# A fused attention and expert kernel: GpSimd's transfers stand behind a small copy of each unit's first quarter of h, and half of the last expert's second weights are reloaded

## The chip, the cores and the metric

The kernel runs on one core of a Trainium2 chip. The metric is the device time of one execution in microseconds (us); a lower one is better. The engines are named as in the profile: PE (TensorE, matmuls), PEld (TensorE's weight loads), DVE (VectorE), ACT (ScalarE), POOL (GpSimd) and SP (SyncE, which here only issues DMAs).

## What is computed

The reference is attention followed by a mixture of experts over the same 4608 tokens (8 sequences of 576, 8 heads of 64, so 512 features a token). Attention looks back over a window of 128 with a linear bias by distance. Then, with x the attention's output:

```python
P = np.exp(x @ w_gate - max)
for _ in range(8):                     # Sinkhorn balance
    P /= P.sum(1, keepdims=True) + 1e-09
    P /= P.sum(0, keepdims=True) + 1e-09
    P *= N / E
for e in range(8):
    h = np.maximum(x @ w1[e], 0.0)     # 512 -> 1024
    out += P[:, e:e + 1] * (h @ w2[e]) # 1024 -> 512
```

Every expert works on every token; P only weights.

## The kernel before

**First stage** (to about 320 us). Attention runs, and in its gaps PE computes experts 0 and 1 for all tokens. Their results y go to DRAM (`ysp`, 36 blocks of 128 tokens for each of the two experts), and so does x (`xd`).

**Second stage** (about 320 us to the end). Experts 2 to 7 run over 18 groups of two token blocks each (256 tokens). One group and one expert make a unit: 108 units, `N`, in the order of `units` (line 905), six (`NE`) to a group. The order of groups is 0 to 7, then 16 and 17 (the tails of the sequences, 64 tokens of each), then 8 to 15.

A unit's first layer (L983, `part`) uses seven block products in place of eight (Strassen): parts a11, s1, s2, a12, s3, s4, a22 accumulate in the PSUM banks A, B and C, and ACT and DVE carry sums between the banks. The result h, [256 tokens x 1024], comes out in four quarters. Quarter 0 is ready after a12 (ACT's relu, L1021, from bank A), quarter 3 after "p+" and quarter 1 after "c+" (DVE's add L1035, then ACT's relu), quarter 2 after a22. Quarters 0 and 3 lie side by side in one of three rotating buffers `hr`, and 1 and 2 in another. One DMA transpose of each pair, `turn_h` (L1027), brings h into `hs` with features on the partitions; SP issues it after p+ and after a22. The buffers called s5y in the profile include the third of the rotation.

The second layer is also a seven-product scheme. DVE adds quarters of the transposed h (L1051, tokens t5 t6 t1 t4 t7), and PE runs the products (L1079, token X) for the unit before, into the banks `psM` (L1079, M in the text). After a group's last unit the products are added to `acc` by DVE (L1123, tokens g1 to g7), in the first units of the next group.

**The written-out order.** All engines work in program order. `plans` (L1250) gives one line of tokens for each of a group's six units; `first` (L1258) replaces the line for some units at the start and for the last unit, N-1. `step` (L1207) reads the tokens. Those that matter here:

- XL0, XL1 (L1236): GpSimd loads the next group's x of block 0 or 1 from `xd` into `xst`. Both blocks share one buffer, which the profile calls consts.
- XT0, XT1 (L919): SP transposes that x into the next group's `xset`.
- Y00, Y01, Y10, Y11 (L1092): GpSimd loads y of expert 0 or 1 (first digit) and block 0 or 1 (second) from `ysp`.
- B00 to B11 (L1097 for expert 0, L1101 for expert 1), "begin": DVE starts acc of a block with P times y, or adds the second y.
- FIN (L1131, L1135): GpSimd stores both blocks of acc of the group before: two stores of 256 KB, or four of 128 KB for a tail group.
- SX (L934 to L936): DVE forms the sums of the next group's x.
- W, F: left-over sums of weights and products of the first stage.

So y loads have one buffer `y[0]`, except y of expert 1 and block 1, which goes to `xst` (`y_at`, L1088). A y load therefore waits for the begin that read the buffer, and XL waits for the XT that read `xst`.

Expert 7's second weights `W2L[7]["all"]` lie in one tile [128, 8 rows of f, 512]. The seven-product scheme overwrites two of their four quarters by sums: q12 (first four f rows, right half) becomes f6, and q21 (last four, left half) f7. The last unit N-1 has no product stream behind it; it ends with ordinary products (`plain`, L1137), which need the original weights. So after expert 7's last Strassen unit the whole tile is loaded again, a f row at a time (`load_w2`, L618), three after each of the units 103 and 104 and two after 105 (L1279).

Of the kernel before, what the change touches and what calls it, by code (L numbers as in the profile page):

```python
# [9 lines left out]
FP16 = mybir.dt.float16  # L10
# [4 lines left out]
def kernel(  # L15
# [10 lines left out]
    nc = tc.nc  # L26
# [17 lines left out]
    SM = RI * P  # L44
    TL = S - SM
# [19 lines left out]
    per = ctx.enter_context(tc.tile_pool(name="per", bufs=1))  # L65
# [186 lines left out]
    if True:  # L252
# [343 lines left out]
        HB = HD // 2  # L596
        NF2 = NFT // 2
# [18 lines left out]
        def load_w2(e, n=0, of=1):  # L616
            k = NFT // of
            nc.gpsimd.dma_start(  # L618
                out=W2L[e]["all"][:, n * k : n * k + k, :],
                in_=moe_w2[e].rearrange("(ft p) d -> p ft d", p=P)[:, n * k : n * k + k, :],  # L620
            )
# [49 lines left out]
        def some(n):  # L671
            for _ in range(min(n, len(todo))):
                todo.pop(0)()
# [44 lines left out]
        for n, (b, kb, u) in enumerate(steps):  # L718
# [111 lines left out]
            if 10 * b + at >= 66:  # L830
                i = 10 * b + at - 66
# [72 lines left out]
        groups = [*range(8), 16, 17, *range(8, 16)]  # L904
        units = [(g, e) for g in groups for e in range(2, E)]
        N = len(units)
        NE = E - 2
# [4 lines left out]
        acc = per.tile([P, 2, HD], FP32, name="acc", tag="xT", bufs=4)  # L912
        xst = [acc.rearrange("p m d -> p (m d)").bitcast(FP16)[:, HD * i : HD * i + HD] for i in range(2)]
# [16 lines left out]
        B11, B21, B12, B22, T1, T3, T2, T4 = range(8)  # L930
# [79 lines left out]
        def rows(n, i):  # L1010

            return hr[(2 * n + i) % 3]

        def quarter(n, slot):
            return rows(n, AT[slot] // 2)[:, AT[slot] % 2]
# [17 lines left out]
        def add_h(n, slot, name):  # L1033
            to = quarter(n, slot)
            nc.vector.tensor_tensor(out=to, in0=psum(name), in1=s5, op=ALU.add)  # L1035
            relu(n, slot, to)
            if slot == 3:
                turn_h(n, 0)

        def sum_h(n, to):  # L1040
            if n < 0:
                return
            t = hs[n % 2]
            x, y, op = {
                5: (1, 3, ALU.add),
                6: (1, 0, ALU.subtract),
                1: (0, 3, ALU.add),
                4: (0, 2, ALU.add),
                7: (3, 2, ALU.subtract),
            }[to]  # L1050
            nc.vector.tensor_tensor(out=t[:, AT.get(to, to)], in0=t[:, AT[x]], in1=t[:, AT[y]], op=op)  # L1051
# [3 lines left out]
        RIGHT = {1: "f1", 2: "q11", 3: "f3", 4: "f4", 5: "q22", 6: "f6", 7: "f7"}  # L1055
        BANK = {3: (0, 0), 4: (0, 1), 2: (1, 0), 6: (1, 1), 5: (2, 0), 7: (2, 1), 1: (3, 0)}
        Ms: dict = {}

        def sum_of(g, m):
            bk = (4 * groups.index(g) + BANK[m][0]) % 5  # L1060
            if bk not in Ms:
                if bk < 4:
                    Ms[bk] = mps.tile([P, 2, 2 * P], FP32, name=f"psM_{bk}")
                else:
                    Ms[bk] = psum("M").rearrange("p (h n) -> p h n", h=2)
            return Ms[bk][:, BANK[m][1], :]
# [6 lines left out]
        def product():  # L1073
            n, m = stream.pop(0)
            g, e = units[n]
            half = BANK[m][1]
            ps = sum_of(g, m)
            for f in range(NF2):
                nc.tensor.matmul(  # L1079
                    out=ps,  # L1080
                    lhsT=hs[n % 2][:, LEFT[m], f, :],
                    rhs=W2L[e][RIGHT[m]][:, f, :],
                    start=(e == 2 and f == 0 and half == 0),
                    stop=(ends(n) and f == NF2 - 1 and (half == 1 or m == 1)),
                    skip_group_check=True,
                )

        def y_at(e, m):  # L1088
            return xst[0] if e == m == 1 else y[0]

        def load_y(g, e, m):
            nc.gpsimd.dma_start(out=y_at(e, m), in_=ysp[e, 2 * g + m])  # L1092
# [29 lines left out]
                    a, p2 = q4[:, lo, :], ps  # L1122
                nc.vector.tensor_tensor(out=a, in0=a, in1=p2, op=op)  # L1123

        def finish(g):
            for m in range(2):
                blk = 2 * g + m
                a = acc[:, m, :]
                if blk < 4 * B:
                    t0 = S * (blk // 4) + P * (blk % 4)  # L1130
                    nc.gpsimd.dma_start(out=out[t0 : t0 + P, :], in_=a)  # L1131
                else:
                    for half in range(2):
                        t0 = S * (2 * (blk - 4 * B) + half) + SM
                        nc.gpsimd.dma_start(out=out[t0 : t0 + TL, :], in_=a[TL * half : TL * half + TL])  # L1135

        def plain(m, name, fh, lo, hi):  # L1137

# [68 lines left out]
        def step(n, plan):  # L1207
            gi = n // NE
            for tok in plan.split():
                if tok == "X":  # L1210
                    product()
                elif tok == "W":
                    some(1)
                elif tok == "F":
                    filler.take()
                elif tok == "p+":
                    add_h(n, 3, "B")
                elif tok == "c+":
                    add_h(n, 1, "C")
                elif tok[0] == "t":  # L1220
                    sum_h(n - 1, int(tok[1]))
                elif tok[0] == "g":
                    last = gi if n == N - 1 else gi - 1
                    if last >= 0:
                        gather(groups[last], int(tok[1]))
                elif tok[0] == "B":
                    begin(groups[gi], int(tok[1]), int(tok[2]))
                elif tok == "FIN":
                    if gi > 0:
                        finish(groups[gi - 1])  # L1230
                elif tok in ("XT0", "XT1"):
                    if gi + 1 < len(groups):
                        turn_x2(gi + 1, int(tok[2]))
                elif tok in ("XL0", "XL1"):
                    if gi + 1 < len(groups):
                        nc.gpsimd.dma_start(out=xst[int(tok[2])], in_=xd[2 * groups[gi + 1] + int(tok[2])])  # L1236
                elif tok == "SX":
                    if gi + 1 < len(groups):
                        sums_x(gi + 1)
                elif tok[0] == "Y":  # L1240
                    load_y(groups[gi], int(tok[1]), int(tok[2]))
                elif tok[0] == "L":
                    slot = int(tok[1])
                    plain_l1(n, slot, {0: "A", 3: "B", 1: "C", 2: "B"}[slot])
                    if slot > 1:
                        turn_h(n, 3 - slot)
                else:
                    part_of(n, tok)

        plans = (  # L1250
# [6 lines left out]
        )  # L1257
        first = {  # L1258
# [4 lines left out]
            N - 1: "a11 X s1 s2 a12 B11 X s3 s4 p+ c+ X X a22 X t5 X X t6 t1 t4 g3 X t7 X g4 X g2 X g6 X g1 g5 g7",  # L1263
        }
        sums_at = {1: 3, 2: 3, 3: 3, 4: 4, 5: 4, 6: 3, 9: 4, 10: 3}
        for n in range(N):
            plan = first.get(n, plans[n % NE])
            one, rest = plan.split(" ", 1)
            step(n, one + " W" * sums_at.get(n, 0) + " " + rest)
            if n == 1:  # L1270
                store()
                aux = per.tile([P, 4, NF2, HB], FP16, name="aux", tag="w2t", bufs=2)
                w2f = per.tile([P, 4, NF2, HB], FP16, name="w2f", tag="w1t", bufs=2)
                todo += sums_of(6, F1_6, w2f[:, 2], w2f[:, 3])
                todo += sums_of(7, aux[:, 0], w2f[:, 0], w2f[:, 1]) + quads_w1(6) + quads_w1(7)
                y.append(per.tile([P, HD], FP16, name="y_e", tag="yo", bufs=YO))
                xst[:] = [consts.rearrange("p a n -> p (a n)").bitcast(FP16)] * 2
                step(n, "Y00 XL0")
            if N - NE + 1 <= n < N - 2:  # L1279
                for i in range(3 * (n - N + NE - 1), min(8, 3 * (n - N + NE))):  # L1280
                    load_w2(E - 1, i, 8)
        plain(1, "A", 1, 0, HD)
        plain(0, "C", 0, 0, HB)
        plain(0, "B", 0, HB, HD)
# [33 lines left out]
```

## Time and profile before

| | us |
|---|---|
| median of 3 timed runs | 1002.11 |
| lowest and highest | 1001.25, 1004.09 |
| the profiled execution | 998.06 |
| its span, first to last instruction | 996.3 |
| PE busy | 979.4 |
| DVE busy | 687.3 |
| ACT busy | 625.5 |
| POOL busy | 192.6 |

The profile shows one execution. A line of a timeline has the start, the time from start to the end of the group of like instructions, the engine, the line of the kernel, what it writes and reads, how many, and in square brackets how long the engine was idle before it and what ended that. A stretch's line has its length, each engine's busy time with the number of its instructions, the granted TensorE clock, the busy share of the 16 DMA engines and the GB/s. In the chain that ended last each piece is named by the engine or DMA that it was spent on. Issue to landing is the time from a DMA's issue to its completion.

In all, 216 transposes of h (SP; `hs<-hr` 144 with a median of 3.3 us to landing, `hs<-s5y` 72 with 3.2), 34 of x from xst (2.6), 72 loads of y (54 with 3.0 and 18 with 2.5), 34 loads of x (2.5), 38 stores (30 of 256 KB with 2.9, 8 of 128 KB with 3.2) and 8 reloads of w2 (128 KB as written, 5.2) are in the second stage.

### The profile page before, as it was taken

The numbers are of one execution on the slowest core, as the hardware profiler recorded it, in microseconds if no ns is written. First come the engines' busy times: TensorE is split into PE (matmuls) and PEld (weight loads), VectorE is DVE, ScalarE is ACT, GpSimd is POOL, SyncE is SP. The second block draws the span as 40 slices with busy tenths as digits, with TensorE's granted clock in tenths as the row PEclk, the third lists the DMA queues.
The fourth block names the chain that finished last, engine by engine and source line by source line (L and its number), as shares of the span: only waits on it lengthen the run. The fifth ranks groups of instructions, "written<-read, shape, count | busy, mean of one in ns | idle before, by whom it ended". The sixth has DMA issues, their size and how long they took to land.

```text
span 996.3 us, 19438 instructions
## 1 busy us (share of the span) xinstructions
PE 979.4 (98%) x7247; PEld 626.0 (63%) x7247; DVE 687.3 (69%) x1546; ACT 625.5 (63%) x1000; POOL 192.6 (19%) x353
## 2 busy tenths in 40 slices
PE   7999999999999999999999999999999999999997
PEld 5645665566544566666666666666666666666665
DVE  5736677675688797676676676676676676776766
ACT  7654555554434656676677677676677676767663
POOL 3315444354010001001111101111101101101120
PEclk9999999999999999999999999999999999999999
DMA  9998999989997667666656656666667656655675
GB/s 244 217 276 208 192 239 224 224 186 185 225 196 159 117 112 145 121 117 148 132 113 138 136 126 131 136 116 128 124 127 133 138 126 129 138 123 122 143 130 119
DMA packets 383454, 155.55 MB, mean 156 GB/s; under 512 B 335296, under 2 KB 372928, under 8 KB 383360
## 3 DMA queue, kind: packets, MB, share of 16 engines
q1 hardware_dynamic: 359680, 110.87, 55.0%
q0 software_dynamic: 23248, 43.27, 20.2%
q8 instruction: 57, 0.93, 0.4%
q14 instruction: 37, 0.30, 0.1%
q10 hardware_dynamic: 432, 0.16, 0.1%
HBM read 78.30 MB, written 23.59 MB: 102 GB/s over the span
## 4 chain that ended last, share of the span: by engine, by line
PE 88%; DMA 6%; DVE 3%; ACT 1%; issue 1%; SPq 1%; POOL 0%; DVEq 0%; POOLq 0%; ACTq 0%
PE psM L1079 30%; PE psB L983 13%; PE psy L159 12%; PE psh L137 9%; PE psA L983 8%; PE psC L983 8%; PE psh L118 3%; DMA hs<-s5y 2%; PE psN L491 1%; PE psS L457 1%; DMA xset<-consts 1%; DMA v<-in_v_dram 1%; DMA consts<-ysp 1%; DVE pt L468 1%; ACT psB L1196 0%
## 5 line engine op out<-in xcount | busy, mean ns | idle before, releaser
L1079 PEld LDWEIGHTS <-hs 128*128 128x128 f16 x2996 | 292.4, 98 | 127.6 <-DVE hs L1051 2.6
L983 PEld LDWEIGHTS <-xset 128*128 128x128 f16 x1484 | 144.8, 98 | 94.0 <-issue 3.8
L1051 DVE TENSOR_TENSOR hs<-hs 128x512 f16<-128x512 f16 x535 | 194.3, 418 | 8.9 <-DMA hs<-hr 4.7
L1079 PE MATMUL psM<-w2l,hs 128*128 128x256 f16 x1440 | 195.6, 273 | 1.2 <-DVE hs L1051 1.2
L159 PE MATMUL psy<-w2t,hT 128*128 128x512 f16 x576 | 135.7, 379 | 0.0
L1021 ACT ACTIVATE hr<-hr,L_sb 128x512 f16<-128x512 f16 x142 | 98.4, 716 | 59.1 <-DVE hr L1035 57.8
L1079 PE MATMUL psM<-more,hs 128*128 128x256 f16 x864 | 121.0, 273 | 1.8 <-DMA hs<-hr 1.8
L1035 DVE TENSOR_TENSOR hr<-psB,s5y 128x512 f16<-128x512 f32 x71 | 49.0, 691 | 94.0 <-PE psB L983 93.2
L983 PE MATMUL psB<-s,xset 128*128 128x512 f16 x356 | 105.7, 378 | 0.8 <-ACT psB L1196 0.4
L983 PE MATMUL psA<-w1l,xset 128*128 128x512 f16 x356 | 105.9, 379 | 0.0
L149 ACT ACTIVATE hT<-psh 128x512 f16<-128x512 f32 (+1 forms) x104 | 60.4, 581 | 70.0 <-PE psh L137 69.9
L137 PE MATMUL psh<-xT,w1t 128*128 128x512 f16 (+1 forms) x448 | 99.0, 364 | 0.0
L463 ACT ACTIVATE pt<-psS 128x1024 f16<-128x1024 f32 x64 | 64.6, 1022 | 49.9 <-PE psS L457 49.3
L159 PEld LDWEIGHTS <-hT 128*128 128x128 f16 x576 | 54.1, 98 | 58.9 <-issue 1.4
L1200 ACT COPY psC<-psB 128x512 f32<-128x512 f32 x106 | 60.4, 570 | 48.8 <-PE psB L983 48.2
L582 DVE CAST yo<-psy 128x512 f16<-128x512 f32 x65 | 44.5, 689 | 50.9 <-PE psy L159 50.3
L1123 DVE TENSOR_TENSOR acc<-acc,psM 128x256 f32<-128x256 f32 (+1 forms) x162 | 77.1, 503 | 2.9 <-PE psM L1079 0.2
L1196 ACT COPY psB<-psA 128x512 f32<-128x512 f32 x106 | 60.4, 570 | 25.9 <-PE psA L983 24.4
L468 DVE TENSOR_TENSOR pt<-pt,mask 128x1024 f16<-128x1024 f16 x64 | 52.1, 814 | 30.4 <-ACT pt L463 30.4
L1198 ACT COPY s5y<-psC 128x512 f32<-128x512 f32 x106 | 62.7, 591 | 6.5 <-PE psC L983 6.5
L137 PEld LDWEIGHTS <-w1t 128*128 128x128 f16 x448 | 41.3, 98 | 37.5 <-issue 0.6
L1131 POOL DMA_DIRECT2D out_dram<-acc x30 | 16.3, 548 | 247.0 <-DVE acc L1123 247.0
(141 smaller groups left out, 1324.0 us busy)
## 6 DMA issues: line engine op xcount, KB each, us to landing
ysp<-yo SPq DMA_DIRECT2D x65, 128.0 KB, 4.2
v<-in_v_dram SPq DMA_DIRECT2D x32, 256.0 KB, 5.0
out_dram<-acc POOLq DMA_DIRECT2D x30, 256.0 KB, 2.9
y_e<-ysp POOLq DMA_DIRECT2D x54, 128.0 KB, 3.0
q<-in_q_dram SPq DMA_DIRECT2D x5, 1024.0 KB, 7.9
k<-in_k_dram SPq DMA_DIRECT2D x5, 1024.0 KB, 9.9
consts<-xd POOLq DMA_DIRECT2D x34, 128.0 KB, 2.5
w1t<-in_moe_w_dram POOLq DMA_DIRECT2D x3, 1024.0 KB, 11.0
```

What stands on the lines that cost most here:

```text
L137: nc.tensor.matmul(out=ps[:, 0:nt], lhsT=w1ts[e][:, dt, P * ft : P * ft + P], rhs=xT[:, at : at + nb, dt, :], start=(dt == 0), stop=(dt == ...
L149: nc.scalar.activation(out=st["hT"][:, ft, 0:nt], in_=ps[:, 0:nt], func=AF.Relu)
L159: nc.tensor.matmul(out=ps, lhsT=st["hT"][:, ft, P * ms : P * ms + P], rhs=w2ts[e][:, ft, :], start=(ft == 0), stop=(ft == NFT - 1),)
L463: nc.scalar.activation(out=pt, in_=ps.rearrange("p a y n -> p (a y) n"), func=AF.Exp, scale=scale)
L468: nc.vector.tensor_tensor(out=pt, in0=pt, in1=mask_of[kb][:, 4 * u : 4 * u + 4, :], op=ALU.mult)
L983: nc.tensor.matmul(out=psum(name), lhsT=xset[n // NE % 2][:, x, P * k : P * k + P], rhs=q[k], start=(start and k == 0), stop=(k == 1), ski ...
L1021: nc.scalar.activation(out=quarter(n, slot), in_=src, func=AF.Relu, scale=P_sb[:, blk, e : e + 1])
L1051: nc.vector.tensor_tensor(out=t[:, AT.get(to, to)], in0=t[:, AT[x]], in1=t[:, AT[y]], op=op)
L1079: nc.tensor.matmul(out=ps, lhsT=hs[n % 2][:, LEFT[m], f, :], rhs=W2L[e][RIGHT[m]][:, f, :], start=(e == 2 and f == 0 and half == 0), stop= ...
L1123: nc.vector.tensor_tensor(out=a, in0=a, in1=p2, op=op)
L1196: nc.scalar.copy(out=psum("B"), in_=psum("A"))
L1198: nc.scalar.copy(out=s5, in_=psum("C"))
```

## The change

A new token G stands in the plans right after a12 in units 0 to 4 of a group (and in the special lines of the first group and the last unit). It is a copy on GpSimd of two elements of each partition from quarter 0 of this unit's h into a new tile `held_at`, which nothing reads. All of GpSimd's transfers of the second stage come right behind a G. The order over the group becomes: unit 0 x of block 0 and Y00; unit 1 x of block 1; unit 2 the store of block 0 (FIN0) and Y01; unit 3 Y10 and the store of block 1 (FIN1); unit 4 Y11. XT0 and XT1 stand behind a22 in units 0 and 1 (units 2 and 3 before). The begins stand in units 3, 4, 5 and 5. y of block 1 now goes to `xst` for both experts, and y of block 0 to `y[0]`. The loads that stood by themselves behind unit 1 are gone.

A new token R, of the last group alone, reloads one half f row of expert 7's second weights: the right half for the first four rows, the left half for the last four, which are the overwritten quarters. Two R stand in unit 1, one in unit 2, one in unit 3, two in unit 4 and two in the last unit. The rest of the tile isn't loaded again.

```diff
+        held_at = per.tile([P, 2], FP16, name="held_at")
...
         def y_at(e, m):
-            return xst[0] if e == m == 1 else y[0]
+            return xst[0] if m else y[0]
...
-        def finish(g):
-            for m in range(2):
-                blk = 2 * g + m
...
+        def finish(g, m):
+            blk = 2 * g + m
...
+        def gate(n):
+
+            nc.gpsimd.tensor_copy(out=held_at, in_=quarter(n, 0)[:, 0:2])
+
+        again = list(range(NFT))
+
+        def load_again():
+
+            ft = again.pop(0)
+            lo = HB if ft < NF2 else 0
+            nc.gpsimd.dma_start(
+                out=W2L[E - 1]["all"][:, ft, lo : lo + HB],
+                in_=moe_w2[E - 1].rearrange("(ft p) d -> p ft d", p=P)[:, ft, lo : lo + HB],
+            )
...
-                elif tok == "FIN":
+                elif tok in ("FIN0", "FIN1"):
                     if gi > 0:
-                        finish(groups[gi - 1])
+                        finish(groups[gi - 1], int(tok[3]))
+                elif tok == "G":
+                    gate(n)
+                elif tok == "R":
+                    if gi == len(groups) - 1:
+                        load_again()
...
         plans = (
-            "a11 s1 X X s2 X a12 s3 s4 p+ X c+ t5 t6 X a22 X t1 t4 X t7",
-            "a11 s1 X g4 X s2 g3 X a12 g6 s3 X s4 p+ X X c+ a22 g5 X t5 t7 g7 t6 t1 t4 g2 Y00 XL0",
-            "a11 s1 X s2 g1 FIN X X a12 s3 p+ s4 X c+ t5 X a22 XT0 XL1 t6 t1 X X t7 t4",
-            "a11 s1 X X s2 B00 Y01 X a12 s3 s4 p+ c+ t5 X t6 X t4 a22 X t1 X XT1 t7 B01",
-            "a11 Y10 Y11 s1 X X s2 X X a12 s3 p+ s4 c+ X t5 t6 t7 X t4 X a22 t1 SX B10",
-            "a11 X X s1 s2 a12 X X s3 B11 s4 p+ c+ X X X t5 t6 t4 t7 a22 t1",
+            "a11 s1 X X s2 X a12 G XL0 Y00 s3 s4 p+ X c+ t5 t6 X a22 XT0 X t1 t4 X t7",
+            "a11 s1 X g4 X s2 g3 X a12 G XL1 R R g6 s3 X s4 p+ X X c+ a22 XT1 g5 X t5 t7 g7 t6 t1 t4 g2",
+            "a11 s1 X s2 g1 X X a12 G FIN0 Y01 R s3 p+ s4 X c+ t5 X a22 t6 t1 X X t7 t4",
+            "a11 s1 X X s2 B00 X a12 G Y10 FIN1 R s3 s4 p+ c+ t5 X t6 X t4 a22 X t1 X t7",
+            "a11 s1 X X s2 B01 X X a12 G Y11 R R s3 p+ s4 c+ X t5 t6 t7 X t4 X a22 t1 SX",
+            "a11 X X s1 s2 B10 a12 X X s3 B11 s4 p+ c+ X X X t5 t6 t4 t7 a22 t1",
         )
         first = {
...
-            4: "L0 Y10 Y11 X X L3 X X L1 X t5 X t6 t4 L2 t7 t1 X SX B10",
-            5: "L0 X X L3 B11 X X L1 X t5 X t6 t4 L2 t7 t1 X",
-            N - 1: "a11 X s1 s2 a12 B11 X s3 s4 p+ c+ X X a22 X t5 X X t6 t1 t4 g3 X t7 X g4 X g2 X g6 X g1 g5 g7",
+            2: "a11 s1 X s2 X X a12 G Y00 XL0 s3 p+ s4 X c+ t5 X a22 XT0 t6 t1 X X t7 t4",
+            3: "a11 s1 X X s2 B00 X a12 G XL1 Y10 s3 s4 p+ c+ t5 X t6 X t4 a22 XT1 X t1 X t7",
+            4: "L0 X X B10 L3 X X L1 G Y01 X t5 X t6 t4 L2 t7 t1 X SX",
+            5: "L0 X X B01 L3 X X L1 G Y11 X t5 X t6 t4 L2 t7 t1 X B11",
+            N - 1: "a11 X s1 s2 B10 a12 G R R B11 X s3 s4 p+ c+ X X a22 X t5 X X t6 t1 t4 g3 X t7 X g4 X g2 X g6 X g1 g5 g7",
         }
...
-                step(n, "Y00 XL0")
-            if N - NE + 1 <= n < N - 2:
-                for i in range(3 * (n - N + NE - 1), min(8, 3 * (n - N + NE))):
-                    load_w2(E - 1, i, 8)
```

More of the change, by code (lines that the diff above doesn't have):

```diff
@@ L1123, in gather @@
                 nc.vector.tensor_tensor(out=a, in0=a, in1=p2, op=op)
-        def finish(g):
-            for m in range(2):
-                blk = 2 * g + m
[L1128 to L1135, printed above, removed]
+        def finish(g, m):
+            blk = 2 * g + m
+            a = acc[:, m, :]
+            if blk < 4 * B:
+                t0 = S * (blk // 4) + P * (blk % 4)
+                nc.gpsimd.dma_start(out=out[t0 : t0 + P, :], in_=a)
+            else:
+                for half in range(2):
+                    t0 = S * (2 * (blk - 4 * B) + half) + SM
+                    nc.gpsimd.dma_start(out=out[t0 : t0 + TL, :], in_=a[TL * half : TL * half + TL])
+        def gate(n):
[8 more added lines that the diff above has]
+            )
         def plain(m, name, fh, lo, hi):
```

## The prediction

> **What bounds the kernel now.** I read the page's engine shares, the chain that ended last, and then the busy times by stretch, because a mean over 996 us says little about one stage.
>
> ```profile
> span 996.3 us, 19438 instructions
> PE 979.4 (98%) x7247; PEld 626.0 (63%) x7247; DVE 687.3 (69%) x1546; ACT 625.5 (63%) x1000; POOL 192.6 (19%) x353
> PE 88%; DMA 6%; DVE 3%; ACT 1%; issue 1%; SPq 1%; POOL 0%; DVEq 0%; POOLq 0%; ACTq 0%
> ```
>
> PE is the bound: 88% of the chain, busy for 98% of the span, at a granted clock of 1.00. Only what PE loses to waits can be won. Where it loses them stands in the stretches of the second stage, cut at about one group of six units each (columns: stretch, its length, busy us of PE, PEld, DVE, ACT, POOL, clock, DMA share, GB/s):
>
> ```profile
> 396.00:432.60 36.60, 35.86 (x249) 23.94 (x247) 25.35 (x59) 25.42 (x43) 4.32 (x8) 1.00 0.73 130
> ...
> 542.00:578.50 36.50, 36.50 (x254) 24.59 (x252) 25.36 (x59) 25.77 (x42) 4.32 (x8) 1.00 0.61 130
> ...
> 651.50:688.00 36.50, 35.45 (x246) 23.68 (x244) 23.32 (x56) 24.35 (x41) 4.84 (x9) 1.00 0.69 127
> 688.00:726.20 38.20, 36.80 (x250) 24.03 (x248) 25.86 (x60) 25.51 (x42) 5.82 (x11) 1.00 0.67 121
> ```
>
> An ordinary group (542 to 578) has PE busy all 36.50 us: 6.08 us a unit, with nothing to win. The losses sit in a few places: about 432, 688 and 720, and the last group. In the timeline of PE the last one reads:
>
> ```profile
> 969.76 0.59 PE L983 MATMUL psB<-w1l,xset 128*128 128x512 f16 x2
> 972.18 1.05 PE L1079 MATMUL psM<-more,hs 128*128 128x256 f16 x8 [1.83 <-DMA hs<-hr]
> 973.07 0.59 PE L983 MATMUL psA<-w1l,xset 128*128 128x512 f16 x2
> 973.50 0.59 PE L983 MATMUL psC<-aux,xset 128*128 128x512 f16 x2
> 975.26 0.94 PE L1079 MATMUL psM<-w2l,hs 128*128 128x256 f16 x7 [1.17 <-DVE hs L1051]
> ```
>
> Two 512-column matmuls take 0.43 us from start to start (973.07 to 973.50), so the start at 972.18 is 1.99 us late and that at 975.26 is 1.33 late: 3.32 us. The same subtraction elsewhere: 0.75 at 431.06; 2.07 at 687.75, 689.11 and 691.65 together; 1.42 from 713 to 723.5; 0.58 at 394 and 397. Sum **8.14 us**. Some 1.0 us more (331, 334, 381, 632, 982) has no transfer in it, and I leave it.
>
> What makes these late, in the chain in order of time:
>
> ```profile
> 425.10 5.92 DMA hs<-s5y
> ...
> 682.26 5.42 DMA consts<-ysp
> ...
> 965.52 9.23 DMA hs<-s5y
> ```
>
> A transpose of h alone lands in 3.2 us (median 3.2 and 3.3). At 425 and 965 one took 5.92 and 9.23, with GpSimd's transfers beside it: in the last group two stores, five w2 loads and a y load issued from 962.52 to 968.0. At 682 a load of y, itself beside two transposes, held a begin on VectorE, behind which the sums for the next h stood. Slower transposes alone do no harm: in ordinary groups the second one of a unit lands after 4.8 us (500.19) and PE doesn't stop. Harm begins between 4.8 and 5.4 us.
>
> **The change, part by part.**
>
> *The gate.* Where is the gap it aims at? Stretches of two ordinary units, same columns:
>
> ```profile
> 485.70:487.40 1.70, 1.70 (x15) 1.24 (x13) 1.67 (x5) 1.70 (x3) 0.04 (x1) 1.00 0.87 308
> 487.40:488.80 1.40, 1.40 (x12) 0.97 (x11) 0.86 (x3) 1.01 (x3) 0.00 (x0) 1.00 0.98 185
> 488.80:490.20 1.40, 1.40 (x11) 0.86 (x10) 0.00 (x0) 0.65 (x2) 0.00 (x0) 1.00 0.99 187
> 490.20:491.00 0.80, 0.80 (x5) 0.35 (x4) 0.14 (x1) 0.65 (x1) 0.00 (x0) 1.00 0.73 168
> 491.00:493.00 2.00, 2.00 (x18) 1.59 (x17) 2.00 (x5) 1.46 (x4) 1.06 (x2) 1.00 0.00 0
> ```
>
> Two stores (issued 484.65 and 485.19) fill the DMA engines from 485.7 to 487.4: 1.05 us from issue to traffic, 0.85 us a store. The transposes issued at 486.25, 487.62 and 488.96 follow until 491.0. Then the DMA engines stand empty for 2 us. ScalarE's relu of the first quarter ends at 491.04 (start 490.35, 0.69), just there; the next transpose is issued at 492.33 and moves from about 493.45 (1.15 later, as 486.25 to 487.4). A gated transfer: relu end 491.04, a copy of two elements, issue at 491.2, traffic from 492.25. The second is issued 0.54 later (POOL's row of one issue) and moves from 492.8. Loads of 128 KB (half a store, about 0.45) and one store fit before 493.45. A third starts at 493.35, beside the transpose, for about 0.5 us: a transpose of 3.2 becomes 3.7, below 4.8. Cost at PE: 0.
>
> The copy itself has no row. Bounds: a memset of 128x16 takes 0.134 us, a copy of 64x512 took 0.60; I take 0.13, the row nearest in size. 90 units hold a gate, on an engine busy for 4.3 of 36.5 us a group: 0. At 0.60 the second transfer would lie half beside a transpose, still under 4.8. Its wait: behind the gate stand only GpSimd's transfers, for which VectorE's begins and the x transposes wait, 4 to 12 us later in the plans, against landings of 2.3 to 3. The buffer of h that it reads is next written by the "c+" of the following unit, some 6.5 us later: no wait.
>
> The Trainium skill speaks against this: "DMA: Bandwidth & Descriptors", Rules for kernel authors, says to issue a DMA early, compute, and wait late, and a gate issues later. By that rule the begins would wait longer; by the rows VectorE's wait for y (41.2 us, 17 times) comes from one y buffer reloaded behind each begin, and the sum goes by the rows. "SBUF — State Buffer" of the Trainium skill, Who interferes with whom, says that GpSimd reading SBUF and a VectorE operation with two SBUF inputs exclude each other; at the gate VectorE runs the adds with one input in PSUM (L1035), and none of the h sums until 492.06. By the rule a gate would lose one sum, 0.42 us, at the worst. No trace here shows it.
>
> *Loads spread and re-paired.* Before, second-block and second-expert y each followed a begin. Now Y00 has a slot three units ahead of its begin, Y01, Y10 and Y11 at least one unit (6.08 us). VectorE's 41.2 + 7.6 us of waits go; VectorE is off the path in ordinary groups, so that is worth only the part inside the 2.07, 1.42, 0.75 and 0.58. The stores are split over two units: the second block's begin then waits for a store issued in the unit before; VectorE reaches it at 493.8 in the unit of the rows above, a store issued at 491.7 lands at 494.6 (2.9), so it waits 0.8 us and is done at 495.1 (0.49), before the next add at 497.37: 0. XT0 and XT1 come two units earlier, behind the second transpose of h as now; SP's queue gets no longer. XL1 and Y01 can't be issued before the x transpose has left xst: 488.96 to 491.94, 2.98 us, which is 0.4 us before the next transpose of h. They are single transfers there, and just fit.
>
> *Tail groups (656 to 726).* Four half stores and a load crowded one unit; now two half stores and a load in each of two: three transfers, 3.7 us a transpose. Gain 2.07 + 1.42.
>
> *Reload of w2.* 8 loads of 64 KB (counted as written) instead of 8 of 128, at most two in a unit. In units 2 to 4 of the last group they are the third transfer: 3.7 us instead of 8 to 9. Gain 3.32. In the very last unit two are issued about 1.4 us before the transpose and land some 3 us later, 1 us before the plain products at 988.99 want them; a miss costs its own length, and I put 0.3 there.
>
> Sum against the profiled execution: 998.06 - 8.14 + 0.3, and 0.2 for third transfers: 990.4. The timed runs' median is 4.05 us longer than that execution. Nothing shows why; that they had more such stalls is possible (these vary from group to group), that it is another thing too, so the gain there is between 7.6 and 11.7. I take the middle, 9.6: **992.5**.
>
> **Rivals.**
> - *The stalls thin out only by half.* XL1 and Y01 go by the landing of an x transpose and not by the gate, with 0.4 us to spare; where one lands 0.5 late, load and transposes of h lengthen each other as at 425, and the third transfers add. For: the cascade at 672 to 688 began so. Against: twelve ordinary groups live with 4.8 us. Half of 8.1: 998.0.
> - *The change moves traffic without parting it*, as where GpSimd comes to its gate already late (plain units of the first group have their first quarter early, so the gate holds nothing). As many bytes beside transposes as before: 1002, no change.
> - *Gate too late, slower.* Place: every unit with two gated transfers. If wake-up, copy and first traffic take 1 us more than I sum (0.60 for the copy is half of that), both run beside both transposes of h. It decides from a landing of 5.4 us on; price then as at 431, 0.75 us, in two units of each of 17 groups: +25, less the 7.6 won: 1020. For: the transposes already fill the engines 0.98. Against: at 491.94 and 492.48 loads were issued 0.7 us later than gated ones would be, and the transposes landed in 3.7.
>
> **How the numbers follow.** Forecast 0.60 (own range 988 to 996), half 0.16, no change 0.11, slower 0.13. The range runs from 988 (all of 11.7 and a little more of waits unseen) to 1002, so that half of the third case is in and under 0.2 is left out. A change under 0.3% (3.0 us) can't be told from none: faster 0.76, same 0.11, slower 0.13.
>
> **What would show it.** Right: PE busy for the full length of every stretch from 400 to 975; group period 36.5 us at 656 to 726; every transpose of h under 4.5 us; VectorE's wait of L1097 for y near 0; GpSimd waiting for the relu of L1021. Wrong: transposes over 5 us, PE waiting for "hs" or for L1035 in ordinary groups, a wait for w2 at the end.

## The result, and the profile after

| | before | after |
|---|---|---|
| median of the timed runs, us | 1002.26 (6 runs) | 992.88 (6 runs) |
| lowest and highest | 1001.25, 1005.98 | 991.27, 993.81 |
| the profiled execution, and its span | 998.06, 996.3 | 993.18, 991.1 |
| second stage of the profiled execution | 676.3 | 669.7 |

The ratio of after to before is 0.9898, with a 95% interval of 0.9879 to 0.9917. A later repeat (e10 below) gave 0.9946 (0.9923 to 0.9969). Lines behind 1058 have moved in after: the gate's copy is L1139, the y load L1093, the begins L1098 and L1102, the second layer's products L1080, the reload L1147, the plain products L1159.

The page of after, its span, engine shares and chain:

```profile
span 991.1 us, 19601 instructions
...
PE 977.8 (99%) x7247; PEld 626.5 (63%) x7247; DVE 691.8 (70%) x1546; ACT 625.6 (63%) x1000; POOL 212.7 (21%) x443
...
PE 92%; DMA 4%; DVE 2%; issue 1%; ACT 0%; POOL 0%; SPq 0%; DVEq 0%; POOLq 0%
```

PE has the same 7247 matmuls, POOL has 90 instructions more (the gates), and DMA's share of the chain fell from 6% to 4%. Busy times by stretch (same columns as before):

```profile
396.00:432.60 36.60, 36.60 (x255) 24.68 (x253) 25.51 (x60) 25.89 (x43) 5.22 (x13) 1.00 0.64 130
...
651.50:688.00 36.50, 36.50 (x253) 24.63 (x252) 25.65 (x60) 25.69 (x43) 6.31 (x15) 1.00 0.73 130
688.00:724.50 36.50, 36.50 (x253) 24.63 (x252) 25.13 (x58) 25.66 (x43) 6.30 (x15) 1.00 0.69 131
```

PE is busy for the full length of all three, those with the tail groups too: no ordinary group holds PE any more. One place is left, in the last unit. The timeline of PE there:

```profile
981.51 1.04 PE L1080 MATMUL psM<-w2l,hs 128*128 128x256 f16 x8
983.78 1.04 PE L1159 MATMUL psA<-w2t,hs 128*128 128x512 f16 x4 [1.24 <-DMA hs<-hr]
```

Eight 256-column matmuls take 8 x 0.109 = 0.87 us from start to start, so the plain products begin 983.78 - 981.51 - 0.87 = 1.40 us late, and what they wait for is a transpose of h. Two reloads of w2 were issued from 977.85 on, behind the last unit's gate and 1 us before the first of its two transposes, which landed after 4.84 and 4.29 us (in before: 3.07 and 3.10).

What the engines waited for between 350 and 960 us (us in all, times, longest), first one line of before, then after:

```profile
DVE acc L1097 <- DMA y_e<-ysp: 38.3, 16, 4.0
```

```profile
POOL held_at L1139 <- ACT hr L1021: 301.1, 51, 10.7
...
DVE acc L1098 <- DMA out_dram<-acc: 27.0, 23, 3.2
...
DVE acc L1102 <- DMA y_e<-ysp: 1.9, 1, 1.9
```

GpSimd now stands at its gates. VectorE's waits for y, 38.3 and 7.6 us in before's same stretch (41.2 and 7.6 over the whole span), are down to 2.8; in their place it waits for the split stores, 1.2 us on average, at a point where PE doesn't need it.

**One measure for all runs.** The first stage has the same code in every kernel here, yet the first matmul of L983 comes between 320.0 and 324.0 us in the 14 profiles (median 321.6; that of before, 320.0, is the earliest). So profiles are compared by their second stage, from that matmul to the end of the span, and by PE's late starts in it: every start-to-start distance beyond 0.217 us a 512-column and 0.109 us a 256-column matmul. The second stage less the late starts is 667.0 to 667.3 in each of the 14, so this sum is what differs. The table's second stages are of one profiled execution each; before and its repeat differ by 0.9 us, after and its repeat by 0.8, the two without a gate by 1.0.

| kernel | second stage | late starts | of these: ordinary groups | last group | timed ratio to before |
|---|---|---|---|---|---|
| before | 676.3 | 9.2 | 4.8 | 3.3 | 1 |
| before again, e8 | 675.4 | 8.2 | 4.6 | 2.6 | one run, 998.65 us |
| after | 669.7 | 2.6 | 0 | 1.4 | 0.9898 |
| after again, e10 | 668.9 | 1.9 | 0 | 0.7 | 0.9946 |
| no gate, e1 | 668.0 | 0.9 | 0 | 0 | 0.9931 (0.9905 to 0.9957) |
| no gate again, e11 | 669.0 | 2.0 | 0 | 1.0 | 0.9921 (0.9892 to 0.9950) |
| slots alone, e9 | 671.4 | 4.2 | 0 | 3.3 | 0.9989 (0.9966 to 1.0012) |
| half reload alone, e3 | 673.1 | 6.0 | 4.5 | 0.6 | 0.9978 (0.9959 to 0.9998) |
| reload earlier, e4 | 668.1 | 1.1 | 0 | 0 | 0.9925 (0.9902 to 0.9947) |
| both stores in one unit, e5 | 670.1 | 3.1 | 0.8 | 1.3 | 0.9921 (0.9893 to 0.9949) |
| whole rows, e6 | 670.4 | 3.4 | 0 | 2.3 | 0.9936 (0.9914 to 0.9959) |
| gate alone, e7 | 683.9 | 16.7 | 14.6 | 1.1 | 1.0072 (1.0044 to 1.0100) |
| late gate in unit 4, e12 | 684.0 | 16.8 | 14.7 | 1.1 | 1.0059 (1.0035 to 1.0083) |
| late gate, e2 | 713.9 | 46.7 | not split | not split | 1.0397 (1.0358 to 1.0436) |

About 1.0 us of each row has no transfer in it, as the prediction left out. The last column's intervals come from the timed runs (4 to 12 of the kernel, 12 to 29 of before beside them).

### The profile page after: what moved, and what is told of

It reads as the page before. It is cut to its first block, busy times and chain, and to the rows that moved or that the text cites. A ratio compares the mean times of both kernels' runs of the same rounds, so it can differ in the third digit from the quotient of the medians.

```text
span 991.1 us, 19601 instructions
## 1 busy us (share of the span) xinstructions
PE 977.8 (99%) x7247; PEld 626.5 (63%) x7247; DVE 691.8 (70%) x1546; ACT 625.6 (63%) x1000; POOL 212.7 (21%) x443
## 4 chain that ended last, share of the span: by engine, by line
PE 92%; DMA 4%; DVE 2%; issue 1%; ACT 0%; POOL 0%; SPq 0%; DVEq 0%; POOLq 0%
PE psM L1080 32%; PE psB L983 14%; PE psy L159 12%; PE psA L983 9%; PE psC L983 9%; PE psh L137 8%; PE psh L118 4%; PE psN L491 1%; DMA q<-in_q_dram 1%; PE psS L457 1%; DMA w2t<-in_moe_w_dram 1%; DMA hs<-hr 1%; DMA v<-in_v_dram 1%; PE psG L551 0%; PE psB L996 0%
## 5 line engine op out<-in xcount | busy, mean ns | idle before, releaser
L1080 PEld LDWEIGHTS <-hs 128*128 128x128 f16 x2996 | 292.9, 98 | 121.6
L983 PEld LDWEIGHTS <-xset 128*128 128x128 f16 x1484 | 144.9, 98 | 91.4 <-issue 1.2
L1051 DVE TENSOR_TENSOR hs<-hs 128x512 f16<-128x512 f16 x535 | 194.4, 418 | 9.8 <-DMA hs<-hr 7.7
L1080 PE MATMUL psM<-w2l,hs 128*128 128x256 f16 x1440 | 195.6, 273 | 0.0
L1080 PE MATMUL psM<-more,hs 128*128 128x256 f16 x864 | 121.0, 273 | 0.0
L1035 DVE TENSOR_TENSOR hr<-psB,s5y 128x512 f16<-128x512 f32 x71 | 49.0, 691 | 90.5 <-PE psB L983 89.7
L983 PE MATMUL psB<-s,xset 128*128 128x512 f16 x356 | 105.7, 378 | 0.3 <-ACT psB L1211 0.2
L983 PE MATMUL psA<-w1l,xset 128*128 128x512 f16 x356 | 105.9, 379 | 0.0
L1139 POOL COPY held_at<-hr 128x2 f16<-128x2 f16 x55 | 10.8, 197 | 347.8 <-ACT hr L1021 347.8
L1124 DVE TENSOR_TENSOR acc<-acc,psM 128x256 f32<-128x256 f32 (+1 forms) x162 | 77.0, 503 | 2.9 <-PE psM L1080 0.2
```

Source lines behind the costliest of these rows:

```text
L983: nc.tensor.matmul(out=psum(name), lhsT=xset[n // NE % 2][:, x, P * k : P * k + P], rhs=q[k], start=(start and k == 0), stop=(k == 1), ski ...
L1080: nc.tensor.matmul(out=ps, lhsT=hs[n % 2][:, LEFT[m], f, :], rhs=W2L[e][RIGHT[m]][:, f, :], start=(e == 2 and f == 0 and half == 0), stop= ...
```

## The experiments

The theory on record was that the gate parts GpSimd's transfers from the transposes of h. Its rival was that the new slots do the work: y and x loaded units ahead of their use, y of block 1 in a buffer of its own, the reload halved and spread. Diffs are against after, unless another kernel is named.

### e1 and e11: no gate

```diff
-                    gate(n)
+                    pass
```

> The changed kernel without the copy: every transfer goes out as soon as its buffer is free, in the changed order. If the gate itself parts the traffic (theory), transposes of h of 5 us and more come back in the tail groups and in the last one, and PE waits with them: 996 to 1000 us. If the gain comes from the new buffers and earlier slots of the y loads and the halved reload (rival), the time stays where the changed kernel is, 992 to 994.5.

Measured: 993.76 us (991.42 to 996.79). VectorE's and GpSimd's waits of this kernel, 350 to 960 us:

```profile
POOL out_dram L1131 <- DVE acc L1124: 67.1, 15, 6.8
...
DVE acc L1098 <- DMA out_dram<-acc: 0.3, 1, 0.3
```

Without gates GpSimd is held by what the transfers themselves need (sums of acc, free buffers), VectorE's new wait for stores falls from 27.0 to 0.3 us, and PE has no late start at a transfer in any ordinary group. The theory falls. Repeated beside after on one chip:

> The changed kernel without the copy once more, on one chip with the changed kernel. Theory now: the gate gives nothing and costs the 1.4 us at the end, so 1 to 2 us faster than the changed kernel or the same within the measurement. Prediction's mechanism: slower by 3 us or more.

Measured: 992.39 us (991.13 to 993.49). No gain from the gate shows; that leaving it out is faster can't be told either, as the intervals of e10 and e11 overlap.

### e10: after again

No edit.

> The changed kernel once more, on one chip with the next run. Second stage 669 to 670.5, time 991 to 994.

Measured: 993.28 us (12 runs), where before gave 999.14 beside it. The change is faster again, by 5.9 us in place of 9.4.

### e9: the slots alone

After's plans and buffers, without gates, with both stores in unit 2 and the whole-tile reload in its old places.

```diff
-                    gate(n)
+                    pass
...
-                        load_again()
+                        pass
...
-            "a11 s1 X s2 g1 X X a12 G FIN0 Y01 R s3 p+ s4 X c+ t5 X a22 t6 t1 X X t7 t4",
-            "a11 s1 X X s2 B00 X a12 G Y10 FIN1 R s3 s4 p+ c+ t5 X t6 X t4 a22 X t1 X t7",
+            "a11 s1 X s2 g1 X X a12 G FIN0 FIN1 Y01 R s3 p+ s4 X c+ t5 X a22 t6 t1 X X t7 t4",
+            "a11 s1 X X s2 B00 X a12 G Y10 R s3 s4 p+ c+ t5 X t6 X t4 a22 X t1 X t7",
...
+            if N - NE + 1 <= n < N - 2:
+                for i in range(3 * (n - N + NE - 1), min(8, 3 * (n - N + NE))):
+                    load_w2(E - 1, i, 8)
```

> The changed plans and y buffers without the gate, with both stores together in unit 2 and the whole-tile reload of the kernel before in its old places: of the change only the earlier slots of the loads (and x transposes) and the second buffer are left. Second stage (first first-layer matmul to the span's end) is 667.1 us plus the late starts of PE in every run so far. Theory now (the distance from a load to its begin is what pays): late starts in ordinary groups vanish, the tail groups keep about 1 us and the last group 2 to 3.5: second stage 670 to 672. Rival (every part is needed): 673 to 676.

Measured: 999.85 us (995.26 to 1002.02), which can't be told from before (999.14 beside it), though the profiled execution took 995.26. Its busy times by stretch:

```profile
396.00:432.60 36.60, 36.60 (x255) 24.71 (x254) 25.33 (x58) 25.88 (x43) 4.31 (x8) 1.00 0.66 131
...
688.00:724.50 36.50, 36.50 (x255) 24.62 (x253) 25.51 (x58) 25.89 (x44) 5.35 (x10) 1.00 0.67 131
```

PE is full in every ordinary group: in this profile the slots alone clear all 4.8 us there. Which part of them does it (the earlier loads, the second buffer, the moved begins and x transposes) wasn't tried one by one. The last group keeps its 3.3 us, with transposes of up to 9.15 us beside the old reload. So the profile and the timed median disagree here. The mean granted clock was below 1.000 (0.996 to 0.998) in 9 of its 12 runs, with a median of 1000.3 us, and 1.000 in three, at 995.3, 995.3 and 996.7; of before's 29 runs beside it 25 were at 1.000, with a median of 999.1. At full clock the slots would then give some 3.8 us, as the profile says, but this split was made after the runs, and whether the kernel or the moment lowered the clock wasn't tried.

How long are the transposes? Of the 180 of units 12 to 101, 23 took over 4.4 us in before, 23 in e9, 22 in e1 and 23 in after: as many, but not the same ones. Over 5 us it is 7 in before, 4 in e9, 1 in e1 and 2 in after. Counted by the DMA packets from 1 us behind a transpose's issue to its landing, all 23 long ones of before and all 22 of e1 had packets of GpSimd's queue (q0) beside them; of after's 23 only four had. The other 19 had an instruction fetch inside (so had 15 of before's and 19 of e1's, beside the packets). So with the gate GpSimd's traffic stays off most of the long ones (though beside more transposes in all, 95 against 83 in e1 and 78 in before), and they stay long; e1 has it beside every long one, and PE doesn't stop.

What changed is where. In unit 4 of a group the first of the two takes up to 5.92 and 6.05 us in before, at 425 and 681, where two of the stalls are, and at most 4.0 in e9 and e1 and 4.3 in after. In unit 2 of e9, in a tail group, both took 6.0 and PE didn't wait. The larger part of before's 4.8 us came through VectorE, where a begin waited for y or for a store and the sums stood behind it. One such place of before, VectorE and then PE:

```profile
719.80 0.49 DVE L1097 TENSOR_SCALAR acc<-y_e,L_sb 128x512 f32<-128x512 f16 x1 [4.00 <-DMA y_e<-ysp]
```

```profile
720.93 0.59 PE L983 MATMUL psB<-w1l,xset 128*128 128x512 f16 x2 [0.75 <-DVE s5y L1035]
```

In e9 no begin waits for y any more.

### e12: only unit 4 gated late

Is unit 4 the place? Its gate moves behind p+, to quarter 3 (about 1.3 us later, so that its one load runs beside both transposes); the rest is after.

```diff
+                elif tok == "H":
+                    nc.gpsimd.tensor_copy(out=held_at, in_=quarter(n, 3)[:, 0:2])
...
-            "a11 s1 X X s2 B01 X X a12 G Y11 R R s3 p+ s4 c+ X t5 t6 t7 X t4 X a22 t1 SX",
+            "a11 s1 X X s2 B01 X X a12 s3 p+ H Y11 R R s4 c+ X t5 t6 t7 X t4 X a22 t1 SX",
```

> The changed kernel with unit 4's gate alone moved behind p+ (a single load there, Y11; two reloads with it in the last group). With all gates late it cost 46 us, and unit 4 had the longest transposes (6.0 to 6.5 us) though it has the fewest transfers. If unit 4 drives that (theory): second stage 690 to 700, transposes of unit 4 near 6. If it needs the other units' late loads and stores too (rival): under 675.

Measured: 1006.11 us (1000.93 to 1009.87), ratio 1.0059 (1.0035 to 1.0083); second stage 684.0, between the two expectations. One load of 128 KB a group in the wrong place (in the last group with two reloads) costs 16.8 - 2.6 = 14.2 us by the profiles, and this profiled execution is the slowest of the ten. A whole case in two timelines; first PE, then VectorE:

```profile
547.08 0.60 PE L1080 MATMUL psM<-w2l,hs 128*128 128x256 f16 x4
548.88 1.05 PE L1080 MATMUL psM<-w2f,hs 128*128 128x256 f16 x8 [1.20 <-DMA hs<-s5y]
550.28 0.59 PE L983 MATMUL psB<-w1t,xset 128*128 128x512 f16 x2 [0.35 <-DVE hr L1035]
```

```profile
548.87 0.75 DVE L1102 SCALAR_TENSOR_TENSOR acc<-consts,L_sb,acc 128x512 f32<-128x512 f16 x1 [3.41 <-DMA consts<-ysp]
549.54 0.68 DVE L1035 TENSOR_TENSOR hr<-psB,s5y 128x512 f16<-128x512 f32 x1
```

The transpose issued at 542.32 landed after 6.51 us, the load of y issued at 542.93 after 5.92. PE starts at 548.88, 1.36 us late (547.08 + 4 x 0.109 = 547.52), released by the transpose. The begin waits 3.41 us for the load, the sum of L1035 stands behind it, and PE is another 0.51 us late on it and 0.38 on ScalarE's copy behind it: 2.25 us, of which 0.89 go through VectorE. In seven groups PE waited for the first transpose itself, each time as long as its landing lay above 5.15 us: 0.68 at 5.83, 0.73 at 5.89, 1.36 at 6.51 (and 0.76 at 5.92 in before). Together that is 6.9 of the 14.7 us lost in ordinary groups. The rest came mostly through VectorE's begin; at landings below 5.15 PE never waited for the transpose itself, and yet 0.65 us were lost at 4.92 (0 at 4.34).

### e2: all gates late

The same H in units 0 to 4 and in units 2 and 3 of the first group; the last unit keeps its G. One of the lines:

```diff
-            "a11 s1 X s2 g1 X X a12 G FIN0 Y01 R s3 p+ s4 X c+ t5 X a22 t6 t1 X X t7 t4",
+            "a11 s1 X s2 g1 X X a12 s3 p+ H FIN0 Y01 R s4 X c+ t5 X a22 t6 t1 X X t7 t4",
```

> The gate moved behind p+, on quarter 3 (the two plain units of the first group and the last unit keep theirs). ScalarE ends that quarter about 1.3 us later than quarter 0, at the moment SP issues the first transpose, so gated traffic begins about 0.7 us into it. Theory (place in the gap decides): transposes of 4 to 5.5 us in every unit with two transfers, PE stalls in some: 995 to 1005. Rival (only buffers and slots matter): 992 to 994.5. The prediction's slower case would be 1010 to 1020.

Measured: 1039.71 us (1037.38 to 1043.92), ratio 1.0397 (1.0358 to 1.0436). Its waits, 350 to 960 us:

```profile
DVE acc L1098 <- DMA out_dram<-acc: 91.8, 28, 5.0
...
DVE acc L1102 <- DMA consts<-ysp: 34.7, 16, 3.4
```

The transposes' median rises from 3.4 to 4.4 us and 41 of 180 take over 4.9 (4 in after); VectorE waits for stores and for y. Against e12, unit 4 is a third of the loss (14.2 of 44.1 us more than after); if the parts add, the rest comes from units 0 to 3.

### e7: the gate alone, on before's plans

Before, with a G in units 1 to 4 and each unit's transfers behind it (XL1 moves from unit 2 to unit 3); begins and buffers as before. Two of the lines, against before:

```diff
-            "a11 s1 X s2 g1 FIN X X a12 s3 p+ s4 X c+ t5 X a22 XT0 XL1 t6 t1 X X t7 t4",
+            "a11 s1 X s2 g1 X X a12 G FIN s3 p+ s4 X c+ t5 X a22 XT0 t6 t1 X X t7 t4",
...
-            "a11 Y10 Y11 s1 X X s2 X X a12 s3 p+ s4 c+ X t5 t6 t7 X t4 X a22 t1 SX B10",
+            "a11 s1 X X s2 X X a12 G Y10 Y11 s3 p+ s4 c+ X t5 t6 t7 X t4 X a22 t1 SX B10",
```

> The kernel before with the gate and nothing else: its loads and stores of units 1 to 4 moved behind a copy of the unit's quarter 0; one y buffer for three of four loads, both stores together, begins and whole-tile reload as before (the first group's plain units and the last unit keep their plans). The run without the gate already speaks against the gate. Theory now (slots between load and begin matter): no gain, second stage 675 to 680, time within 0.5% of the kernel before or slower. The prediction's own mechanism (the gate parts the traffic): 671 to 673, some 5 us faster.

Measured: 1007.14 us (1005.77 to 1012.07), ratio 1.0072 (1.0044 to 1.0100). VectorE's wait for the y buffer, 350 to 960 us:

```profile
DVE acc L1098 <- DMA y_e<-ysp: 52.6, 16, 4.8
```

Its wait for y_e grows from 38.3 us in before's same stretch to 52.6, that for consts from 7.6 to 21.5, and PE loses 14.6 us in ordinary groups. A gated load that a begin wants soon makes the begin late. This is what the rule of the Trainium skill says ("DMA: Bandwidth & Descriptors", Rules for kernel authors: issue a DMA early, compute, wait late), and this run agrees.

### e3, e4 and e6: the reload

e3 is before, with half f rows reloaded in the old places:

```diff
-                    load_w2(E - 1, i, 8)
+                    lo = HB if i < NF2 else 0
+                    nc.gpsimd.dma_start(
+                        out=W2L[E - 1]["all"][:, i, lo : lo + HB],
+                        in_=moe_w2[E - 1].rearrange("(ft p) d -> p ft d", p=P)[:, i, lo : lo + HB],
+                    )
```

> The kernel before with one part of the change alone: the reload of expert 7's second weights halved, in the old places, the other half not loaded. Theory: the last group's 3.3 us fall to 1 or 2, the other stalls (4.8 us in the profiled execution) stay: 999.5 to 1001. Rival (the reload is most of the gain): 996 to 999.

Measured: 999.70 us (12 runs), ratio 0.9978 (0.9959 to 0.9998); the last group's late starts fall from 3.3 to 0.6 us. By the profiles e9's 4.8 us and these 2.7 make 7.5, 0.9 more than the whole change's 6.6, which loses 1.4 us again at the end. The timed ratios don't add up so: 0.9989 and 0.9978 against 0.9946 or 0.9898 for the whole.

e4 issues all of it before the last unit:

```diff
-            "a11 s1 X g4 X s2 g3 X a12 G XL1 R R g6 s3 X s4 p+ X X c+ a22 XT1 g5 X t5 t7 g7 t6 t1 t4 g2",
+            "a11 s1 X g4 X s2 g3 X a12 G XL1 R R R R g6 s3 X s4 p+ X X c+ a22 XT1 g5 X t5 t7 g7 t6 t1 t4 g2",
...
-            N - 1: "a11 X s1 s2 B10 a12 G R R B11 X s3 s4 p+ c+ X X a22 X t5 X X t6 t1 t4 g3 X t7 X g4 X g2 X g6 X g1 g5 g7",
+            N - 1: "a11 X s1 s2 B10 a12 G B11 X s3 s4 p+ c+ X X a22 X t5 X X t6 t1 t4 g3 X t7 X g4 X g2 X g6 X g1 g5 g7",
```

> The changed kernel with the last unit's two reloads moved to unit 1 of the last group (four there, one, one and two in units 2 to 4, none in the last unit). In the changed kernel's profile PE starts the plain products 1.4 us late (1.24 of it idle), waiting for a transpose of 4.84 us beside these two loads. Theory: the transpose falls to 3.2 and 1.4 us go: 991.5, ratio to the changed kernel 0.9986. Rival: that transpose is late for another reason, or four reloads in unit 1 stall that unit: 992.5 to 994.

Measured: 993.50 us (991.79 to 994.17). In its profile the last transpose lands after 3.15 us and the 1.40 us are gone. The timed median doesn't show it. That the reloads alone made the last transposes long isn't shown, though: in e11 the last reload had landed at 973.01, and the transposes issued at 977.55 and 978.87 took 4.47 and 3.91 us all the same:

```profile
982.07 1.04 PE L1159 MATMUL psA<-w2t,hs 128*128 128x512 f16 x4 [0.87 <-DMA hs<-hr]
```

The same instruction fetch of 16 KB runs there in every profile. In after, e11, e2 and e5 it falls 1.9 to 2.9 us behind the issue of the first of the two, which takes 4.47 to 4.88 us; in e1 and e4, without a reload beside, it falls 0.2 to 0.3 us behind, and the transpose takes 3.07 and 3.15. In e10 it falls as early, with two reloads beside, and the transpose takes 4.11. No run parts the two.

e6 reloads whole rows in after's places:

```diff
-            lo = HB if ft < NF2 else 0
...
-                out=W2L[E - 1]["all"][:, ft, lo : lo + HB],
-                in_=moe_w2[E - 1].rearrange("(ft p) d -> p ft d", p=P)[:, ft, lo : lo + HB],
+                out=W2L[E - 1]["all"][:, ft, :],
+                in_=moe_w2[E - 1].rearrange("(ft p) d -> p ft d", p=P)[:, ft, :],
```

> The changed kernel with whole rows of w2 reloaded in the new slots, twice the bytes. If half the bytes matter (theory), the last group's transposes pass 5.4 us and PE waits 1 to 3 us more: second stage 671 to 673. If the slots alone matter (rival): 669.7 to 670.5.

Measured: 994.36 us (993.6 to 997.55), with 2.3 us late in the last group where after has 1.4. 2.0 us of it stand in front of the plain products: spread whole rows hold PE in the middle of the group no longer, but two of them now stand at the end. The second stage, 670.4, is the rival's number, and in time this can't be told from after. Halving in the old places (e3) does more, 3.3 to 0.6, than spreading whole rows, 3.3 to 2.3; each is one profile.

### e5: both stores in unit 2

```diff
-            "a11 s1 X s2 g1 X X a12 G FIN0 Y01 R s3 p+ s4 X c+ t5 X a22 t6 t1 X X t7 t4",
-            "a11 s1 X X s2 B00 X a12 G Y10 FIN1 R s3 s4 p+ c+ t5 X t6 X t4 a22 X t1 X t7",
+            "a11 s1 X s2 g1 X X a12 G FIN0 FIN1 Y01 R s3 p+ s4 X c+ t5 X a22 t6 t1 X X t7 t4",
+            "a11 s1 X X s2 B00 X a12 G Y10 R s3 s4 p+ c+ t5 X t6 X t4 a22 X t1 X t7",
```

> The changed kernel with both blocks' stores again in unit 2, behind the gate, with Y01 behind them; all else as changed. Times below are of the second stage alone, from the first first-layer matmul of that stage to the end of the profiled span (before 676.3, changed 669.7, without the gate 668.0), since the first stage differs by up to 4 us between executions of the same code. If the split of the stores is what empties units 56 to 63 (theory), the tail groups stall again by 1.5 to 3.5 us: 671 to 673. If the y loads' earlier slots did it (rival): 669.5 to 670.

Measured: 993.06 us (990.91 to 996.27): 0.8 us late in a tail group, where five transfers meet in one unit, and nothing elsewhere. Not to be told from after in time.

### e8: before again

No edit of before.

> The kernel before, unchanged, profiled once more. The first profiled execution took 998.06 where the timed ones took 1002. Theory: both its stages were short by luck; here the first stage takes 321 to 324 us (320.0 there) and the second has 8 to 12 us of late starts (9.2 there), at other places. Rival: something outside the span.

Measured: 998.65 us, late starts of 8.2 us in all, partly in other places (395.7, 579, 764, 905). The stalls of before are no fixed list; their sum is much the same.

## Why the prediction was right, and where it was wrong

**The sum held, the mechanism didn't.** 992.5 was forecast and 992.88 measured, but the step that credited the gate failed. The prediction said that the transfers, parted from the transposes, would leave these under 4.5 us, and that PE's stalls would go with that. Of 180 transposes 22 took longer in after, up to 5.27, most of them with no traffic of GpSimd beside them; PE's stalls are gone without the gate, with that traffic beside every long one (e1, e9, e11); and the gate on before's plans costs 0.7% (e7). By the profiles what pays is that y is loaded units ahead of its begin, and that less stands beside the first transpose of unit 4, plus the smaller reload. The timed runs show no part of the gate, and 0.2% for the smaller reload (e3, its interval just short of 1); the slots' part they don't show (e9). The text listed the slots as one part, "loads spread and re-paired", and called VectorE's 41.2 + 7.6 us of waits worth only their share in the late starts; that share was the larger part, and e12 shows both ways at work, 1.36 us through the transpose and 0.89 through the begin.

**The 8.14 us.** Before's late starts at transfers fell from 8.14 to 1.40, all that is left in the last unit. The second stage fell by 6.6 us: 8.14 - 1.40, less 0.13 more in the starts without a transfer. The 7.6 us forecast were 1.0 too many.

**The mis-sized term** is the last unit's reload: 0.3 us put, 1.40 measured (0.67 in e10, none in e4). The prediction asked whether the reload would land in time for the plain products, and it did (980.82, against 983.78). What it left out is that the last two transposes can themselves be late, 4.8 and 4.3 us for 3.1, with nothing behind them to cover it. How much of that the two reloads beside them do stays open: with reloads and an early fetch 0.67 us were lost (e10), with a late fetch and no reload in flight 1.03 (e11).

**The median.** The middle of 7.6 and 11.7 us gave 9.6. The first comparison measured 9.4, the repeat 5.9, nearer the 6.6 us of the profiles. Of the 4.05 us by which before's median lay above its profiled execution, 1.6 can be the early first stage of that execution (320.0 against a median of 321.6 over the 14 profiles). The rest stays open, so that the forecast met 992.88 this closely is partly luck.

**The gate's price.** From the relu's end to the first issue it took 0.66 us in the median of 90 (0.13 to wake, 0.18 copy, 0.34 to the issue) where 0.16 was put. It did no harm: the first transposes of unit 4 still landed within 4.3 us. The split stores make VectorE wait 1.2 us, 23 times, for a forecast of 0.8.

**The rivals.** "Half" and "no change" didn't come. "Gate too late" was right in kind, and shown by e2 and e12: a phase of 1.3 us turns the gain into a loss. Its price was too low, 1020 against 1039.71, since it counted 0.75 us in two units of a group, and up to 2.32 in one unit was measured (e12, at a landing of 6.59). Its threshold, a landing of 4.8 to 5.4 us, was right for the transpose itself: 5.15 for the first one of unit 4. What it left out is the begin behind a late load of y, which made PE late from landings of some 4.4 us on.

## What to carry to other kernels

Ask first which waits a rearrangement ends, and try its parts one by one: here the new synchronisation was the visible part of the change, and the unseen one, loads issued units ahead and into a second buffer, cleared the stalls in the profile without it. Where an engine's slack differs from unit to unit, place transfers by the unit that has least, and look at the first thing that it waits for. And at the very end of a kernel there is no later work to hide a late transfer: ask there separately what its last transfers hold up.

## What the runs showed of the hardware

**A tiny copy can stand behind VectorE.** Copies of after's gate, at quarter 0, and of e2's gate, at quarter 3 (shortest, median and longest in ns, then the first and last start):

```profile
L1139 POOL COPY held_at<-hr x55: 178/184/719, 338.1 to 977.4; 128x2 f16<-128x2 f16 x55
```

```profile
L1249 POOL COPY held_at<-hr x53: 178/422/3441, 340.9 to 1010.3; 128x2 f16<-128x2 f16 x53
```

These lines hold 55 of after's 90 copies and 53 of e2's; the others read h from a buffer named s5y. In after 85 of the 90 run beside the adds of L1035, which read PSUM, and take 0.184 us. In e2, 59 run beside a sum of L1051, with both inputs in SBUF, and take 0.42 us in the median, a sum's own length (0.418); beside the additions of L1124, which read PSUM, or an idle VectorE, they take 0.184. The longest, 3.44 us, began in a row of eleven such sums without a gap. "SBUF — State Buffer" of the Trainium skill, Who interferes with whom, says that GpSimd and VectorE share a port pair under an exclusive lock; these runs agree, and the prediction's bound of 0.42 us at the worst holds for a lone sum alone: in after too one copy took 1.19 us, beside a row of weight sums (L658).

**Long transposes with an instruction fetch inside.** DMA traffic of after around the second transpose of unit 4, first at 609.83, then at 828.83:

```profile
q1 hardware_dynamic: 2112, 0.52, 65.3%
q8 instruction: 1, 0.02, 1.3%
q14 instruction: 1, 0.01, 0.4%
issues: line engine op xcount, KB each, median us to landing
hs<-hr SPq DMA_TRANSPOSE x1, 4.9
```

```profile
q1 hardware_dynamic: 2096, 0.52, 80.9%
issues: line engine op xcount, KB each, median us to landing
hs<-hr SPq DMA_TRANSPOSE x1, 3.3
```

With fetches of 16 and 8 KB inside it, the transpose takes 4.9 us, without them 3.3. Second transposes of unit 4 take about 4.8 us until 800 us and 3.2 later, in after and in e9 alike. No line of q0 stands in either view, so nothing of GpSimd's moved beside these two. Of after's 23 transposes over 4.4 us 19 are of this kind. But a fetch isn't enough: in before 21 transposes had one between issue and landing and no packet of GpSimd's beside them (counted as for e9), and none took over 3.53 us. No run moved a fetch, so it isn't shown as the cause.

**The granted clock at the start.** In e3's profile the first 40 us were granted 0.96, with 356 matmuls done; in before 1.00 and 393. Its second stage begins 4.0 us later; e4 has 0.96 and 358 there, and begins 3.5 us later. Busy times of the first 40 us, e3 and then before:

```profile
0.00:40.00 40.00, 31.96 (x356) 23.64 (x357) 23.31 (x53) 27.59 (x49) 12.55 (x29) 0.96 1.07 227
```

```profile
0.00:40.00 40.00, 33.87 (x393) 25.06 (x394) 25.68 (x61) 29.60 (x52) 12.66 (x29) 1.00 1.11 233
```

A later second stage comes at full clock too (323.8 in e12), so the clock explains only a part of the spread.
